# GpSimd's exponent steps as 64-bit integer adds, and its other arithmetic on VectorE

## The chip, the core and the metric

The kernel runs on one core of a Trainium2 chip. A core has five engines with instruction queues of their own: TensorE (PE in the profile, its weight loads PEld) multiplies matrices into PSUM; ScalarE (ACT) computes exponentials and GELU; VectorE (DVE) does elementwise work and empties PSUM; GpSimd (POOL) does elementwise work in SBUF; SyncE (SP) issues DMAs. The metric is the device time of one execution in microseconds. Three runs of the kernel before took 747.74, 748.66 and 748.88 us; the median is 748.66 us.

## What is computed

A token mixer with 2048 tokens of 512 numbers. One branch is softmax attention with 32 heads of 16 numbers each; the other is a small MLP with shifted channels; a gate mixes the two.

```python
def reference(A_x, A_wqkv, A_wo, B_x, B_w1, B_w2, B_w3, B_w4, gate_w):
    ...
        scores = jnp.einsum("bhqd,bhkd->bhqk", q, k) * (Dh ** -0.5)
        p = _softmax(scores, axis=-1)
        o = jnp.einsum("bhqk,bhkd->bhqd", p, v)
        return (lambda x, *d: x.transpose(*d))(o, 0, 2, 1, 3).reshape(B, S, D) @ wo
    ...
        h = _gelu(_layernorm(x, axis=-1) @ w1)
        ...
        x1 = x + hs
        h2 = _gelu(_layernorm(x1, axis=-1) @ w3) @ w4
        return x1 + h2
    x = A_x
    g = _sigmoid((x * gate_w).sum(-1, keepdims=True))
    a = _A_ref(x, A_wqkv, A_wo)
    b = _B_ref(x, B_w1, B_w2, B_w3, B_w4)
    return g * a + (1 - g) * b
```

The scores are 32 matrices of 2048 x 2048 numbers, and the exponential of each of them is the bulk of the elementwise work.

## The kernel before

**Units and blocks.** The attention is cut into 32 units: 512 queries (a chunk `c`) times four heads (`u`). A unit has 16 key tiles of 128 keys, and for each of them one block of 128 x 512 scores per head: 64 blocks, 2048 in all. A score matmul uses 32 rows of the array and an attention matmul 32 columns, so that up to four of a kind run beside each other.

**Two ways to the exponential.** Most blocks lie two or three together in a PSUM tile `stage`, and one ScalarE instruction (`expo`, L1228) takes the exponentials into `ring`; TensorE then multiplies them with the values (`attend_block`, L1241). The other blocks go four by four (a key tile's four heads, in the text a *quad*) through integer arithmetic, in `whole` (L1024). Each block is scored into a PSUM tile `dsc`; VectorE adds a constant and writes int16 (`dump`, L1048): the bits of a bfloat16 number near the exponential. For a better value the sum of four such numbers is taken, each with a shifted exponent and its own weight: three *steps* (`step`, L1090) make the shifted copies of the 128 x 2048 int16 tile, on VectorE (L1113) or on GpSimd (L1111), and TensorE multiplies all four terms with the values, weighted (`vw`) or plain (`vp`). So a quad has up to four dumps, three steps and four attention groups, where ScalarE's way has one attention group.

**Slots.** After the first 34, a score slot has three blocks: three for ScalarE, or two for ScalarE and one for a quad. Two `stage` tiles alternate. The MLP's matmuls, the projections and the output products are fitted between the slots (`job_run`, `proj`, L301), a few matmuls at a time; where nothing is at hand, TensorE multiplies by a tile of zeros (`fill`, L1565).

**A planner writes the order.** Python code at the end (`pe_option`, `option`, `run`) simulates the four engines at build time with a cost for each operation and appends each instruction to its engine's queue in the order of that simulation. On the chip the queues run in that order, with semaphore waits between engines. The costs stand in the `post` calls: 0.157 + 0.533 a block for a dump (L1158), 0.69 for a step on VectorE, 1.9 on GpSimd (`offer`, L1133), 1.28 for a scaling of an output on GpSimd (L1344).

**The limits.** `RULES` (L171) gives limits for each unit, with `USUAL` (L170) for the rest. `DLIM` is how far VectorE's planned backlog may reach when a block is still given to a quad (L777); `MAXD` how many blocks of a unit may go that way; `CHAINS` how many quads may be open. A step is offered to both engines (`offer`, L1142): GpSimd takes it if VectorE's backlog is at least `BACK` and the quad has fewer than `PMAX` steps on GpSimd; VectorE takes it whenever it comes to it. The first step of a quad always goes to VectorE (`opens`, L1125).

**The shared port.** The planner keeps GpSimd's operations and those of VectorE that are posted as `shared` apart in time (L1585, L1591-1593), and `behind` (L264) makes GpSimd's instruction wait for the last such VectorE instruction.

**GpSimd's other work.** The normalized rows `xn` (`norm`, L438), the inverse roots for the two layer norms (`root`, L427 to L430), the second half of `qT` (`odd`, L357), the weighted values `vw` (`weigh`, L366), the scaling of each unit's output by its denominators (`scale`, L1353; the last three units on VectorE, L1351), the gate's last step (`affine`, L486), and one of the last four output tiles (`gate_act`, L1455 to L1469).

Of the kernel before, what the change touches and what calls it, by code (L numbers as in the profile page):

```python
# [33 lines left out]
def kernel(  # L34
# [126 lines left out]
    for j in range(4):  # L161
# [8 lines left out]
    USUAL = {'WIDE': 1, 'NEED': 14, 'AHEAD': 12, 'HURRY': 32, 'DLIM': 1.2, 'MANY': 8, 'PTS': 5, 'CHAINS': 2, 'MAXD': 28, 'PMAX': 3, 'BACK': 1.2, 'SHORT': 1}  # L170
    RULES = {  # L171
        1: {'NEED': 22, 'AHEAD': 20, 'HURRY': 8, 'DLIM': 1.5, 'CHAINS': 5, 'PMAX': 1, 'BACK': 0.0, 'SHORT': 2},
        2: {'NEED': 8, 'AHEAD': 8, 'HURRY': 14, 'DLIM': 0.9, 'MANY': 4, 'PTS': 7, 'CHAINS': 3, 'MAXD': 20, 'PMAX': 2, 'BACK': 0.9, 'SHORT': 3},
        3: {'NEED': 16, 'AHEAD': 20, 'PTS': 6, 'BACK': 0.6},
        4: {'PTS': 7, 'BACK': 0.9},
        5: {'PTS': 4},
        6: {'HURRY': 14, 'MANY': 6, 'MAXD': 24, 'PMAX': 1},
        10: {'NEED': 16, 'AHEAD': 20, 'HURRY': 18, 'DLIM': 2.5, 'MANY': 10, 'PTS': 7, 'MAXD': 24, 'PMAX': 2, 'BACK': -1, 'SHORT': 2},
        12: {'NEED': 32, 'MANY': 6, 'BACK': 0.9},
        13: {'NEED': 12, 'HURRY': 24, 'MANY': 6, 'SHORT': 2},  # L180
        16: {'NEED': 8, 'AHEAD': 16, 'HURRY': 8, 'DLIM': 1.8, 'MANY': 10, 'PTS': 6, 'CHAINS': 3, 'BACK': 0.3},
        17: {'DLIM': 0.6, 'CHAINS': 5},
        18: {'AHEAD': 24, 'HURRY': 0, 'MANY': 6, 'PTS': 4, 'CHAINS': 5, 'SHORT': -1},
        20: {'HURRY': 8, 'MANY': 3},
        22: {'NEED': 10, 'AHEAD': 8, 'HURRY': 8, 'DLIM': 2.5, 'PTS': 3, 'PMAX': 1, 'BACK': 0.6, 'SHORT': -1},
        23: {'NEED': 28, 'AHEAD': 8, 'DLIM': 0.9, 'MANY': 6, 'PTS': 3, 'CHAINS': 5, 'MAXD': 20, 'PMAX': 1, 'BACK': 1.6, 'SHORT': -1},
        24: {'NEED': 18, 'MANY': 6},
        25: {'NEED': 10, 'AHEAD': 16, 'HURRY': 0, 'DLIM': 3.0, 'MANY': 5, 'CHAINS': 3, 'PMAX': 1, 'BACK': 1.6, 'SHORT': 3},
        26: {'NEED': 20, 'AHEAD': 20, 'HURRY': 18, 'MANY': 5, 'PTS': 6, 'CHAINS': 3, 'MAXD': 20, 'PMAX': 2, 'BACK': 0.6, 'SHORT': 2},
        27: {'CHAINS': 4},  # L190
        28: {'NEED': 20, 'AHEAD': 8, 'HURRY': 64, 'DLIM': 0.6, 'MANY': 6, 'PTS': 6, 'CHAINS': 4, 'BACK': 0.6, 'SHORT': 4},
        29: {'NEED': 12, 'AHEAD': 24, 'HURRY': 24, 'MANY': 6, 'PTS': 6, 'CHAINS': 5, 'MAXD': 20, 'PMAX': 2, 'BACK': 1.6, 'SHORT': 2},
        30: {'NEED': 28, 'HURRY': 8, 'DLIM': 1.5, 'MANY': 5, 'CHAINS': 4, 'MAXD': 16, 'BACK': 1.6, 'SHORT': 0},
        31: {'NEED': 16, 'AHEAD': 8, 'HURRY': 4, 'DLIM': 0.9, 'MANY': 10, 'PTS': 4, 'CHAINS': 5, 'MAXD': 20, 'PMAX': 1},
# [29 lines left out]
    GAP = 0.3  # L224
    AGE = 4.0
# [117 lines left out]
    def q_proj(c, G):  # L343
# [4 lines left out]
        def fn(end):  # L348
            qT = qpool.tile([P, 2, CH], BF16, tag="qT", name="qT")
            qTs[(c, G)] = qT  # L350
            nc.vector.tensor_scalar(out=qT[:, 0, :], in0=ps[:], scalar1=QS, scalar2=None, op0=ALU.mult)  # L351
            at["q", c, 2 * G] = end
            post("pool", 1, 0.69, odd, end + 0.04)

        def odd(end):
            qT = qTs[(c, G)]
            behind(nc.gpsimd.tensor_scalar(out=qT[:, 1, :], in0=qT[:, 0, :], scalar1=second[:], scalar2=0.0, op0=ALU.mult, op1=ALU.add))  # L357
# [5 lines left out]
    def weigh(t, half, end):  # L363
        heads = slice(half * H // 2, (half + 1) * H // 2)
        for i in range(2):
            nc.gpsimd.tensor_scalar(out=vw[t][:, i, heads, :], in0=vp[t - 1][:, heads, :], scalar1=WEIGHTS[i + 2], scalar2=0.0,  # L366
                                    op0=ALU.mult, op1=ALU.add)
        at["vw", half] = end

    def v_proj(t, half):  # L370
# [13 lines left out]
        def fn(end):  # L384
            nc.vector.tensor_copy(out=dst[:, heads, 1:DH + 1], in_=ps[:, 0:width].rearrange("p (h d) -> p h d", d=DH))
# [17 lines left out]
    offsets = [const.tile([P, NT], F32, name=f"offset{n}") for n in range(2)]  # L403
# [5 lines left out]
    def ln_stats(n, t):  # L409
# [12 lines left out]
        def plus(end):  # L422
            post("pool", 0, 1.9, root, end + 0.04)

        def root(end):
# [3 lines left out]
            nc.gpsimd.tensor_tensor(out=offsets[n][:, tt], in0=mvs[n][:, tt, 0], in1=rstds[n][:, tt], op=ALU.mult)  # L429
            nc.gpsimd.tensor_scalar(out=offsets[n][:, tt], in0=offsets[n][:, tt], scalar1=-1.0, scalar2=0.0, op0=ALU.mult, op1=ALU.add)  # L430

        aside(0.17, plus)

    def norm(n, c):
        def normed(t):
            def fn(end):
                xn = xnpool.tile([P, D], BF16, tag="xn", name="xn")
                behind(nc.gpsimd.tensor_scalar(out=xn[:], in0=x_sb[t][:], scalar1=rstds[n][:, t:t + 1],  # L438
                                               scalar2=offsets[n][:, t:t + 1], op0=ALU.mult, op1=ALU.add))
# [4 lines left out]
        for t in range(4 * c, 4 * c + 4):  # L444
            post("pool", 1, 0.775, normed(t), all_at(("rstd", n, c), "xnfree"))
# [39 lines left out]
    def affine(end):  # L485
        nc.gpsimd.tensor_scalar(out=g_fin[:], in0=g_t[:], scalar1=0.5, scalar2=0.5, op0=ALU.mult, op1=ALU.add)  # L486
# [1193 lines left out]
```

## Time and profile before

| what | us |
|---|---|
| median of three runs | 748.66 |
| profiled execution, its own time | 748.4 |
| its span, from the first to the last instruction | 746.6 |
| GpSimd busy | 339.3 |
| steps on GpSimd, 123 of them | 233.7 |
| steps on VectorE, 303 of them | 207.9 |
| exponentials on ScalarE, 683 instructions | 679.5 |

Busy times of an engine are unions of its instructions' spans. Neighbouring instructions of one engine overlap in part, so an engine's rate is read from the starts of instructions that follow each other, not from their durations. The granted TensorE clock was 1.0 throughout.

### The profile page before, as it was taken

How to read it: one execution, taken by the hardware profiler on the slowest of the kernel's cores; microseconds unless marked ns; L12 is line 12 of the kernel's file. 1: busy time of each engine (PE TensorE's matmuls, PEld its weight loads, DVE VectorE, ACT ScalarE, POOL GpSimd, SP SyncE). 2: the span in 40 equal slices, each digit the busy share in tenths (PEclk: the TensorE clock that was granted, in tenths of full speed). 3: DMA queues.
4: the chain of work that ended last, by engine and by line, in shares of the span. 5: the costliest groups of instructions: out<-in, count | busy, mean ns of one | idle time of the engine just before them, and what ended most of it. 6: DMA issues, size and time to landing. Idle time of an engine off the chain costs nothing.

```text
span 746.6 us, 23400 instructions
## 1 busy us (share of the span) xinstructions
PE 730.8 (98%) x9866; PEld 230.9 (31%) x9866; DVE 683.6 (92%) x1178; ACT 729.8 (98%) x731; POOL 339.3 (45%) x295
## 2 busy tenths in 40 slices
PE   8999999999999999999999999999999999999997
PEld 4333332322332333332222332222322222322232
DVE  5799999999999998689999989999799999999994
ACT  6999999999999999999999999999999999999995
POOL 3734426444455456325564533454335455345420
PEclk9999999999999999999999999999999999999999
DMA  9400006201130060050001020000201000000011
GB/s 197 124 17 13 13 21 104 47 26 41 34 119 21 18 142 10 21 49 16 20 28 34 14 47 18 19 12 15 56 25 33 6 21 20 26 18 20 15 34 42
DMA packets 52306, 29.03 MB, mean 39 GB/s; under 512 B 36712, under 2 KB 47720, under 8 KB 52200
## 3 DMA queue, kind: packets, MB, share of 16 engines
q1 hardware_dynamic: 51240, 27.00, 15.1%
q8 instruction: 77, 1.26, 0.7%
q10 hardware_dynamic: 960, 0.52, 0.2%
q14 instruction: 29, 0.24, 0.1%
HBM read 17.17 MB, written 2.35 MB: 26 GB/s over the span
## 4 chain that ended last, share of the span: by engine, by line
PE 45%; ACT 41%; issue 10%; DVE 4%; DVEq 0%; ACTq 0%
ACT ring L1228 35%; PE acc L1241 16%; PE stage L831 14%; PE ps L301 6%; ACT pt L1228 3%; PE ps_o L301 2%; PE ps_y L301 2%; PE stage L301 1%; ACT g2T L1205 1%; DVE quad L1048 1%; ACT hT L1205 1%; ACT g2T L1208 1%; DVE xT L1048 1%; PE acc L301 1%; PE ps_q L301 1%
## 5 line engine op out<-in xcount | busy, mean ns | idle before, releaser
L1228 ACT ACTIVATE ring<-stage 128x1024 bf16<-128x1024 f32 (+1 forms) x649 | 648.3, 1159 | 1.9 <-PE dsc L831 0.5
L831 PE MATMUL stage<-qT,kT 32*128 32x512 bf16 (+2 forms) x1530 | 269.1, 380 | 6.0 <-ACT ring L1228 3.1
L831 PE MATMUL dsc<-qT,kT 16*128 16x512 bf16 (+1 forms) x542 | 208.2, 384 | 0.1
L831 PEld LDWEIGHTS <-kT 32*128 32x128 bf16 (+1 forms) x2072 | 77.0, 91 | 278.4 <-issue 250.9
L1048 DVE TENSOR_SCALAR quad<-dsc 128x512 int16<-128x512 f32 x235 | 155.1, 683 | 7.5 <-PE dsc L831 6.5
L1241 PE MATMUL acc<-ring,vp 128*17 128x512 bf16 (+3 forms) x1436 | 133.1, 378 | 1.3 <-DVE accsb L1402 0.5
L1111 POOL TENSOR_SCALAR quad<-quad 128x2048 int16<-128x2048 int16 x36 | 68.4, 1901 | 67.9 <-DVE quad L1113 22.9
L1048 DVE TENSOR_SCALAR more<-dsc 128x512 int16<-128x512 f32 x129 | 85.4, 683 | 5.5 <-PE dsc L831 4.5
L1048 DVE TENSOR_SCALAR xT<-dsc 128x512 int16<-128x512 f32 x122 | 80.5, 683 | 3.1 <-PE dsc L831 2.6
L1241 PEld LDWEIGHTS <-vp 128*17 128x17 bf16 (+1 forms) x2640 | 56.4, 89 | 81.4 <-issue 62.2
L301 PE MATMUL ps<-w,g2T 128*32 128x512 bf16 x896 | 70.2, 383 | 0.0
L1111 POOL TENSOR_SCALAR more<-more 128x2048 int16<-128x2048 int16 x20 | 38.0, 1900 | 56.8 <-DVE quad L1113 30.7
L1353 POOL TENSOR_TENSOR oT<-accsb,bcs 128x512 bf16<-128x512 f32 x29 | 37.1, 1279 | 44.6 <-DVE quad L1113 22.2
L301 PE MATMUL ps_y<-xnT,w 128*32 128x512 bf16 x704 | 54.8, 383 | 0.3 <-DVE qT L351 0.3
L1113 DVE TENSOR_SCALAR quad<-quad 128x2048 int16<-128x2048 int16 x61 | 45.6, 748 | 0.7 <-PE acc L1241 0.7
L1241 PE MATMUL acc<-quad,vp 128*17 128x512 bf16 x492 | 45.8, 381 | 0.0
L1111 POOL TENSOR_SCALAR xT<-xT 128x2048 int16<-128x2048 int16 x16 | 30.4, 1901 | 33.1 <-DVE xT L1113 7.0
L1241 PE MATMUL acc<-quad,vw 128*17 128x512 bf16 x468 | 45.2, 381 | 0.0
L1111 POOL TENSOR_SCALAR more<-quad 128x2048 int16<-128x2048 int16 x14 | 26.6, 1901 | 27.7 <-DVE quad L1113 8.1
L1048 DVE TENSOR_SCALAR lent<-dsc 128x512 int16<-128x512 f32 x56 | 37.2, 682 | 1.5 <-PE dsc L831 1.2
L1241 PEld LDWEIGHTS <-vw 128*17 128x17 bf16 x1136 | 27.8, 88 | 33.7 <-issue 25.7
L301 PEld LDWEIGHTS <-w 128*32 128x32 bf16 x1152 | 26.1, 95 | 35.3 <-issue 19.4
(146 smaller groups left out, 943.8 us busy)
## 6 DMA issues: line engine op xcount, KB each, us to landing
bcs<-rec_d SPq DMA_DIRECT2D x31, 256.0 KB
w<-in_B_w_dram SPq DMA_DIRECT2D x2, 1792.0 KB
x_sb<-in_A_x_dram SPq DMA_DIRECT2D x14, 128.0 KB
oT<-oT SPq DMA_DIRECT2D x112, 16.0 KB
out_dram<-ot SPq DMA_DIRECT2D x12, 128.0 KB
w<-in_B_w_dram SPq DMA_DIRECT2D x2, 512.0 KB
wkv<-in_A_wqkv_dram SPq DMA_DIRECT2D x1, 512.0 KB
wo_all<-in_A_wo_dram SPq DMA_DIRECT2D x8, 64.0 KB
```

What stands on the lines that cost most here:

```text
L301: nc.tensor.matmul(out[j:j + 32, :], lhsT=lhsT[:, j:j + 32], rhs=rhs, tile_position=(0, j), **kwargs)
L831: nc.tensor.matmul(out, lhsT=kT[G][32 * j:32 * j + K, cc, o:o + P], rhs=qTs[(c, G)][32 * j:32 * j + K, a, lo:hi], start=True, stop=True, t ...
L1048: nc.vector.tensor_scalar(out=bits[:, r:r + wide, :], in0=dsc.rearrange("p (a c) -> p a c", c=CH), scalar1=SHIFT, scalar2=LOWEST, op0=ALU. ...
L1111: behind(nc.gpsimd.tensor_scalar(out=to, in0=base["tile"], scalar1=1.0, scalar2=shift, op0=ALU.mult, op1=ALU.add))
L1113: fast["ins"] = nc.vector.tensor_scalar(out=to, in0=base["tile"], scalar1=shift, scalar2=None, op0=ALU.add)
L1205: nc.scalar.activation(out=part, in_=part, func=ACT.Gelu_apprx_tanh)
L1208: nc.scalar.activation(out=dst, in_=stages.pop(k)[:, 0:len(ms) * CH].rearrange("p (a c) -> p a c", c=CH), func=ACT.Gelu_apprx_tanh)
L1228: nc.scalar.activation(out=pt[:, 0:w], in_=stages.pop(k)[:, 0:w], func=ACT.Exp, scale=LN2 / 128.0)
L1241: nc.tensor.matmul(accs[n][32 * j:32 * j + M, lo:hi], lhsT=lhsT, rhs=p, start=(kt == 0), stop=(kt == NT - 1), skip_group_check=True, tile_ ...
L1353: behind(nc.gpsimd.tensor_tensor(out=oT, in0=tiles["accsb"][:], in1=tiles["bcs"][:], op=ALU.mult))
```

## The change

Five things change.

1. A step on GpSimd is one `int64_add` over the tile seen as 512 64-bit words per partition, with the shift repeated in the four 16-bit lanes, in place of a `tensor_scalar` over 2048 int16 elements. Every lane stays positive, so nothing is carried from lane to lane. The planner's cost for it is 1.07 in place of 1.9.
2. GpSimd's other arithmetic goes to VectorE: `odd`, `weigh`, `norm`, `affine`, every `scale` and the last tile's `gate`. The second layer norm's inverse roots are computed on VectorE by an integer first guess and four Newton rounds (19 small instructions for four tiles of rows); the first layer norm's stay on GpSimd, without the two instructions for `offset`.
3. `scale` is posted to VectorE without the mark `shared`.
4. VectorE leaves a step to GpSimd if GpSimd is free less than `KEEP` = 0.6 us after VectorE, as long as the quad has fewer than `PMAX` = 3 steps there.
5. The limits of units 1 to 31 are one set.

```diff
+        1: {'NEED': 10, 'AHEAD': 8, 'HURRY': 0, 'DLIM': 0.6, 'MANY': 10, 'PTS': 6, 'CHAINS': 6, 'MAXD': 24, 'BACK': 0.6, 'SHORT': 0, 'KEEP': 0.6},
...
+    PSTEP = 1.07
...
+    def words(tile):
+        return tile.rearrange("p a c -> p (a c)").bitcast(mybir.dt.int64)
...
-            post("pool", 1, 0.69, odd, end + 0.04)
+            post("vector", 1, 0.41, odd, end + 0.04, True)
...
-                post("pool", 1, 0.95, lambda end: weigh(t, half, end), end + 0.04)
+                post("vector", 1, 0.5, lambda end: weigh(t, half, end), end + 0.04, True)
...
+        def newton(end):
+            at["rstd", n, t // 4] = end
+            y, z = rstds[n][:, tt], root_z[:]
+            half = root_x[:]
+            nc.vector.tensor_scalar(out=half, in0=mvs[n][:, tt, 1], scalar1=EPS, scalar2=None, op0=ALU.add)
+            nc.vector.tensor_scalar(out=z.bitcast(I32), in0=half.bitcast(I32), scalar1=1, scalar2=None, op0=ALU.logical_shift_right)
+            nc.vector.tensor_scalar(out=y.bitcast(I32), in0=z.bitcast(I32), scalar1=-1.0, scalar2=float(MAGIC), op0=ALU.mult, op1=ALU.add)
+            for _ in range(4):
+                nc.vector.tensor_tensor(out=z, in0=y, in1=y, op=ALU.mult)
+                nc.vector.tensor_tensor(out=z, in0=z, in1=half, op=ALU.mult)
+                nc.vector.tensor_scalar(out=z, in0=z, scalar1=-0.5, scalar2=1.5, op0=ALU.mult, op1=ALU.add)
+                nc.vector.tensor_tensor(out=y, in0=y, in1=z, op=ALU.mult)
+        if n:
+            aside(1.6, newton)
+        else:
+            aside(0.17, plus)
...
-                behind(nc.gpsimd.tensor_scalar(out=xn[:], in0=x_sb[t][:], scalar1=rstds[n][:, t:t + 1],
-                                               scalar2=offsets[n][:, t:t + 1], op0=ALU.mult, op1=ALU.add))
+                fast["ins"] = nc.vector.tensor_scalar(out=xn[:], in0=x_sb[t][:], scalar1=mvs[n][:, t, 0:1],
+                                                      scalar2=rstds[n][:, t:t + 1], op0=ALU.subtract, op1=ALU.mult)
...
-                behind(nc.gpsimd.tensor_scalar(out=to, in0=base["tile"], scalar1=1.0, scalar2=shift, op0=ALU.mult, op1=ALU.add))
+                behind(nc.gpsimd.int64_add(out=words(to), in0=words(base["tile"]), in1=int(shift) * 0x0001000100010001))
...
-            offer("pool", 1.9, end)
+            offer("pool", PSTEP, end)
...
+                elif chain["pool"] < rule("PMAX") and free["pool"] < free["vector"] + rule("KEEP"):
+                    return None
...
-            post("vector" if late else "pool", 0 if late else 3, 0.68 if late else 1.28, scale, lambda: landed if oroom or u % 2 else None, True)
+            post("vector", 0 if late else 3, 0.68, scale, lambda: landed if oroom or u % 2 else None)
...
-            if j:
-                post("vector", -5 * r + (r == 0), 0.75, gate, free["pe"] + 0.2)
-            else:
-                post("act", 1, 0.6, gate_act, free["pe"] + 0.2)
+            post("vector", -5 * r + (r == 0), 0.75, gate, free["pe"] + 0.2)
```

More of the change, by code (lines that the diff above doesn't have):

```diff
@@ L402 @@
     rstds = [const.tile([P, NT], F32, name=f"rstd{n}") for n in range(2)]
-    offsets = [const.tile([P, NT], F32, name=f"offset{n}") for n in range(2)]
+    MAGIC = 0x5f3759df
+    root_x, root_z = (const.tile([P, 4], F32, name=f"root_{k}") for k in "xz")
     xns = {}
@@ L1349, in scale @@
             oT = oroom.popleft() if padded else npool.tile([P, CH], BF16, tag="oT", name="oT")[:]
[L1350 to L1353 removed]
+            nc.vector.tensor_tensor(out=oT, in0=tiles["accsb"][:], in1=tiles["bcs"][:], op=ALU.mult)
             at["o", c, u] = end
```

81 lines of the change are left out of this document (36 added, 45 removed).

## The prediction

> **What bounds the kernel now.** I read the page first, its busy times and the engines' shares of the chain that ended last.
>
> ```profile
> PE 730.8 (98%) x9866; PEld 230.9 (31%) x9866; DVE 683.6 (92%) x1178; ACT 729.8 (98%) x731; POOL 339.3 (45%) x295
> PE 45%; ACT 41%; issue 10%; DVE 4%; DVEq 0%; ACTq 0%
> ```
>
> TensorE and ScalarE share the chain, and VectorE is nearly full too. Busy shares alone don't say who has room, so the second view is ScalarE's groups by shape, and the third a stretch of its timeline.
>
> ```profile
> L1228 ACT ACTIVATE ring<-stage 128x1024 bf16<-128x1024 f32 x535 | 505.0, 1082 | 1.5 <-PE dsc L831 0.5
> L1228 ACT ACTIVATE ring<-stage 128x1536 bf16<-128x1536 f32 x114 | 163.0, 1517 | 0.5 <-PE stage L831 0.3
> L1228 ACT ACTIVATE pt<-stage 128x1024 bf16<-128x1024 f32 x34 | 31.4, 1091 | 0.6 <-PE stage L831 0.5
> 359.86 8.50 ACT L1228 ACTIVATE ring<-stage 128x1024 bf16<-128x1024 f32 x9
> ```
>
> Idle time ahead of the exponentials is 2.6 us in all. Nine of them in 8.50 us with a last one of 1.08 start every (8.50 - 1.08) / 8 = 0.93 us. A third block costs 1517 - 1082 = 0.435 us more. At these prices ScalarE's 569 instructions of two blocks and 114 of three need 569 x 0.93 + 114 x 1.365 = 685 us; the rest of its 729.8 busy us is GELUs and table loads. **ScalarE sets the time, and the time falls only where blocks are taken from it**: 4 x 0.435 = 1.74 us for each further quad. The blocks that it has: 535 x 2 + 114 x 3 + 34 x 2 = 1480 of 2048, so 568 blocks, 142 quads, go the other way.
>
> Who could take more? The fourth view is the windows, one stage of the first half and one of the second, then the same stages for the multiplications by zeros alone (TensorE).
>
> ```profile
> 150.00:200.00 50.00, 49.64 (x641) 14.82 (x640) 49.01 (x83) 49.98 (x52) 22.62 (x18) 1.00 0.17 38
> 350.00:400.00 50.00, 49.52 (x661) 14.25 (x657) 48.27 (x80) 49.85 (x51) 27.31 (x19) 1.00 0.10 31
> ```
>
> ```profile
> 150.00:200.00 50.00, 4.95 (x52) 1.00 0.17 38
> 350.00:400.00 50.00, 0.39 (x4) 1.00 0.10 31
> 0.00:747.00 747.00, 28.77 (x328) 1.00 0.16 39
> ```
>
> VectorE (third engine column) is busy 49.0 and 48.3 of 50 us: it has no room in either half. TensorE has some in the first half, where it multiplies by zeros 13 times (52 instructions, four beside each other), and almost none in the second (once). So VectorE's relief is what the change can turn into quads, and in the second half TensorE may not allow it.
>
> **The change part by part.** The steps first: their number and price on the two engines, the prices of GpSimd's other work, and the starts of VectorE's steps.
>
> ```profile
> 0.00:747.00 747.00, 207.89 (x303) 1.00 0.16 39
> 0.00:747.00 747.00, 233.74 (x123) 1.00 0.16 39
> L1111 POOL TENSOR_SCALAR quad<-quad 128x2048 int16<-128x2048 int16 x36 | 68.4, 1901 | 67.9 <-DVE quad L1113 22.9 <-DVE xT L1113 15.9 <-DVE more L1113 12.0
> L1353 POOL TENSOR_TENSOR oT<-accsb,bcs 128x512 bf16<-128x512 f32 x29 | 37.1, 1279 | 44.6 <-DVE quad L1113 22.2 <-DMA bcs<-rec_d 7.5 <-DVE mv L417 6.1
> L438 POOL TENSOR_SCALAR xn<-x_sb,rstd,offset 128x512 bf16<-128x512 bf16 x32 | 24.4, 772 | 13.2 <-issue 5.7 <-DVE lent L1113 4.5 <-DVE quad L1113 1.9
> L366 POOL TENSOR_SCALAR vw<-vp 128x272 bf16<-128x272 bf16 x24 | 12.1, 504 | 8.1 <-DVE g_raw L390 7.0
> L357 POOL TENSOR_SCALAR qT<-qT,second 128x512 bf16<-128x512 bf16 x15 | 10.4, 692 | 11.4 <-DVE qT L351 6.2 <-DVE more L1113 2.6 <-DVE quad L1113 1.2
> 269.20 0.69 DVE L1113 TENSOR_SCALAR xT<-quad 128x2048 int16<-128x2048 int16 x1
> 269.80 0.69 DVE L1113 TENSOR_SCALAR more<-more 128x2048 int16<-128x2048 int16 x1
> 270.40 0.69 DVE L1113 TENSOR_SCALAR quad<-quad 128x2048 int16<-128x2048 int16 x1
> ```
>
> 303 + 123 = 426 steps are three for each of 142 quads, as counted above. A VectorE step takes 0.60 us of the queue.
>
> *Price of a 64-bit step.* No row shows one. Bounds: 0.69 us (L357, as many elements as there are words, a quarter of the bytes) and 1.90 us (L1111, the same bytes). The planner's costs for the operations above are 1.9, 1.28, 0.775 and 0.69 against 1.901, 1.279, 0.772 and 0.692 in the rows, so its 1.07 for the new one is likely a measured figure too, and it lies between the bounds. I take it.
>
> *Steps off VectorE.* The first step of a quad stays there: 142. Of the other 284 the new rule leaves to GpSimd those for which GpSimd is free within 0.6 us of VectorE. GpSimd would be busy 40% of the time, so I take nine in ten, 256; VectorE keeps 170. That is 133 fewer, 133 x 0.60 = 79.8 us off VectorE. Ends: all 284 (161 fewer, 96.6 us) and six in ten (90 fewer, 54 us). GpSimd: 339.3 - 233.7 - 84.0 (the four other rows) + 256 x 1.07 = 296 us; it has the room.
>
> *Work onto VectorE.* Rows of VectorE for the nearest operations:
>
> ```profile
> L1351 DVE TENSOR_TENSOR oT<-accsb,bcs 128x512 bf16<-128x512 f32 x2 | 1.4, 684 | 0.4 <-DMA bcs<-rec_d 0.4
> L390 DVE COPY g_raw<-ps_v 128x1 f32<-128x1 f32 x16 | 2.4, 147 | 0.0
> L1113 DVE TENSOR_SCALAR xT<-xT 128x2048 int16<-128x2048 int16 x20 | 13.8, 694 | 0.2
> L385 DVE CAST vp<-ps_v 128x256 bf16<-128x256 f32 x32 | 13.3, 415 | 3.5 <-PE ps_v L301 3.3
> L1504 DVE TENSOR_SCALAR qT<-ps_q,mask 128x256 bf16<-128x256 f32 x1 | 0.5, 484 | 0.7 <-PE ps_q L1499 0.7
> L417 DVE BATCH_NORM_AGGREGATE mv<-st 128x2 f32<-128x6 f32 x32 | 5.6, 174 | 0.2
> ```
>
> The 29 scalings: 684 ns is 0.60 in the queue (0.09 overlaps, as for the steps), 17.4 us. `xn` and `qT`, 47 of 512 columns from SBUF: between one column (147) and 2048 (694), on the line 0.28 us, with 0.07 added for scalars read from memory (484 against 415) and 0.09 overlapped: 0.26, 12.2 us (ends 0.06 and 0.60: 3 and 28 us). `vw`, 24 of 272 columns: 0.13, 3.1 us. The Newton rounds, 4 x 19 instructions, each on the result of the one before: nothing overlaps, 0.174 and a little for the hand-over, 0.20: 15.2 us, where the planner has 4 x 1.6 = 6.4. Together 47.9 us.
>
> *The unmarked scalings.* `scale` reads two SBUF tiles and is no longer kept apart from GpSimd. If the two cannot run together, it waits for the step under way: from nothing to 1.07 us each, 0 to 31 us. GpSimd busy 40% of the time and half a step on average would be 0.21; I take 0.25, 7.3 us. The Trainium skill, "SBUF — State Buffer", section "Who interferes with whom", speaks against the edit: a VectorE instruction with two SBUF inputs contends with a GpSimd instruction that reads SBUF, and the loser blocks wholly. By that rule the 7.3 us stay in, without it they go, which is worth 2.7 us at the end; the two L1351 above can't show it.
>
> *What that buys.* Net relief 79.8 - 47.9 - 7.3 = 24.6 us of VectorE. A further quad costs it four dumps and 1.2 steps:
>
> ```profile
> L1048 DVE TENSOR_SCALAR quad<-dsc 128x512 int16<-128x512 f32 x235 | 155.1, 683 | 7.5 <-PE dsc L831 6.5
> ```
>
> (4 + 1.2) x 0.60 = 3.1 us; and it shortens the run by 1.74, of which VectorE was using 92%: 1.6. So 24.6 / 4.7 = 5.2 quads at an equally full VectorE: **-9.1 us**. TensorE pays three more attention groups a quad, 0.22 us each by their starts:
>
> ```profile
> 299.72 0.39 PE L1241 MATMUL acc<-more,vp 128*17 128x512 bf16 x4
> 299.94 0.39 PE L1241 MATMUL acc<-quad,vw 128*17 128x512 bf16 x4
> ```
>
> 5.2 x 0.66 = 3.4 us, which the 82 groups of zeros (18 us) hide in the first half. Without that cover it is the first rival.
>
> *What the Newton rounds hold up.* Each run of 19 takes 3.8 us of VectorE's queue where 1.6 are planned. Behind it stand dumps, and the score slot after next waits for them, then ScalarE. 4 x 2.2 = 8.8 us if all is passed on, 0 if VectorE was ahead; I take a third: **+2.9 us**.
>
> *The end.* The last work is the gate of the last tiles.
>
> ```profile
> 740.67 1.27 POOL L1461 TENSOR_TENSOR ring<-ring,parts 128x512 bf16<-128x512 f32 x1 [21.12 <-ACT ring L1458]
> 740.74 2.07 DVE L1451 SCALAR_TENSOR_TENSOR ring<-end,g_fin,parts 128x512 bf16<-128x512 f32 x3
> ```
>
> Four in place of three on VectorE, 0.69 each with overlap 0.66: **+0.7 us** (at worst; nothing if the fourth fits ahead).
>
> *The one set of limits.* I cost it at nothing, as the count of quads follows from VectorE's room above; its price if it is not so is the second rival.
>
> Sum: 746.6 - 9.1 + 2.9 + 0.7 = 741.1 us of span; the execution's 748.4 is 1.8 longer than its span, so 742.9, **743 us**. That execution is 0.26 us under the median of 748.66. With all steps on GpSimd, no port wait and Newton at 6.4 us: (96.6 - 39.1) / 4.6 = 12.5 quads, -21.8 us, 727; with `xn` and `qT` at their lower end two quads more, 724.
>
> **The rivals.** *No room on TensorE.* The zeros are gone after 300 us, so TensorE can carry more attention groups only in the first half. Then half of the 9.1 us comes, and with the 3.6 lost above the time is 748.4 - 4.5 + 3.6 = 747.5, no change. For it: the two window rows above. Against it: the MLP's matmuls can slide forward into the room.
>
> *A backlog limit that refuses quads* (slower). `DLIM` is now 0.6 everywhere; a single dump of 0.68 in the queue exceeds it. Before, units 17 and 28 had 0.6 and units 24 and 29 had 1.2; their dumps, in windows between the copies of the accumulators (line 1048), in that order:
>
> ```profile
> 401.20:422.50 21.30, 11.72 (x18) 1.00 0.07 21
> 656.60:678.10 21.50, 11.96 (x19) 1.00 0.05 16
> 563.40:584.80 21.40, 13.02 (x20) 1.00 0.10 31
> 678.10:700.60 22.50, 15.09 (x24) 1.00 0.07 20
> ```
>
> 0.86 dumps per us under 0.6, 1.00 under 1.2: 14% fewer. If the 71 quads of the second half lose that, 10 x 1.74 = 17.4 us, and with 3.6 the time is 769; with part of it made good by the freed VectorE, 765. It decides as soon as quads fall below 140, where the 3.6 us are no longer paid for. Against it: a less loaded VectorE seldom has 0.6 us of backlog.
>
> *A dear or late 64-bit step.* TensorE's order is fixed with a step of 1.07 and 0.25 of hold. At 1.9 each of 256 steps is up to 0.58 late, at most 148 us; it begins to hurt above 1.3. The Trainium skill, "GPSIMD Engine Reference", section "2.1 Instruction dispatch", has about 6 us for the first call of a freshly loaded routine, which by an estimate from that page would make 749 if nothing hid it; no run here shows it, and GpSimd idles 7.17 us ahead of its first step (row below).
>
> ```profile
> 44.63 1.90 POOL L1111 TENSOR_SCALAR lent<-quad 128x2048 int16<-128x2048 int16 x1 [7.17 <-DVE quad L1113]
> ```
>
> *The steps don't move.* GpSimd still takes a step only when VectorE's backlog is 0.6 or more. If VectorE kept its 303, the 47.9 us would cost 48 / 4.7 = 10 quads: +17.4, with 3.6 769 us.
>
> **How the numbers follow.** Forecast, with its better cases, 54%; no room on TensorE 14%; backlog limit 24%; dear step 5%; steps stay 3%. Under 0.2% (1.5 us) a measurement can't tell the time from no change. So faster 0.54, same 0.14, slower 0.32. The range reaches from the best case of the forecast (724, a little under for unknown prices) to the backlog rival: 722 to 768; perhaps 4% lie below and 14% above.
>
> **What would show it.** Right: about 147 quads (588 dumped blocks), ScalarE's instructions of three blocks fewer than 114, some 256 rows of GpSimd at about 1.07 us, VectorE's steps near 170 to 180, VectorE still about 92% busy. Wrong: fewer than 140 quads; TensorE waiting for GpSimd's steps; idle time of ScalarE well over 2.6 us, above all at the Newton rounds; more multiplications by zeros, which would say that TensorE, too, was left with nothing to do.

## The result: slower by 2.8%

The changed kernel took 770.16 us (median of four runs, 768.23 to 793.91) beside 748.27 us for the kernel before on the same chip: a ratio of 1.0284, 95% interval 1.0248 to 1.032. The forecast was 743 us. Executions more than 1.5% above the fastest of their kernel, all at a lower granted clock, are left out of the ratios: here the one of 793.91 us, and below five of ten near 771 us of the run with one round alone and two of four, 777 and 783 us, of the run in five pieces. The profiled execution took 768.44 us with a span of 766.7, which is 20.1 us longer than before.

The page's busy times and shares of the chain, of the changed kernel, then ScalarE's exponentials by shape (count, busy us, mean ns, idle us ahead of them and what ended it):

```profile
PE 736.3 (96%) x9833; PEld 222.9 (29%) x9834; DVE 662.2 (86%) x1220; ACT 723.7 (94%) x728; POOL 319.5 (42%) x338
PE 52%; ACT 26%; DVE 12%; issue 8%; DMA 1%; POOL 1%; SPq 0%; DVEq 0%; ACTq 0%; POOLq 0%
```

```profile
L1256 ACT ACTIVATE ring<-stage 128x1024 bf16<-128x1024 f32 x549 | 518.4, 1059 | 16.1 <-PE dsc L857 14.9
L1256 ACT ACTIVATE ring<-stage 128x1536 bf16<-128x1536 f32 x98 | 141.0, 1481 | 5.8 <-PE stage L857 5.5
L1256 ACT ACTIVATE pt<-stage 128x1024 bf16<-128x1024 f32 x34 | 31.6, 1084 | 2.2 <-PE stage L857 2.2
```

ScalarE was relieved as forecast: 549 x 2 + 98 x 3 + 34 x 2 = 1460 blocks, so 588 blocks or 147 quads go the other way, five more than before, and its busy time falls by 6.1 us. But it stands idle 24.1 us ahead of the exponentials, where it stood 2.6, nearly all of it waiting for score matmuls.

The steps on GpSimd, those on VectorE and the multiplications by zeros, each a window over the whole span with busy us and count; then the operations that moved to VectorE:

```profile
0.00:766.70 766.70, 308.02 (x292) 0.98 0.16 38
```

```profile
0.00:766.70 766.70, 102.81 (x149) 0.98 0.16 38
```

```profile
0.00:766.70 766.70, 21.41 (x236) 5.91 (x236) 0.21 (x1) 0.98 0.16 38
```

```profile
L1378 DVE TENSOR_TENSOR oT<-accsb,bcs 128x512 bf16<-128x512 f32 x31 | 25.5, 824 | 0.0
L464 DVE TENSOR_SCALAR xn<-x_sb,mv,rstd 128x512 bf16<-128x512 bf16 x32 | 12.6, 404 | 0.0
L369 DVE TENSOR_SCALAR qT<-qT,second 128x512 bf16<-128x512 bf16 x15 | 5.1, 343 | 0.0
L378 DVE TENSOR_SCALAR vw<-vp 128x272 bf16<-128x272 bf16 x24 | 4.8, 246 | 0.0
```

GpSimd made 292 steps at 308.02 / 292 = 1.05 us, and VectorE's steps fell from 303 to 149. So the steps moved as the change says. The time went in two other places.

**The start.** GpSimd's timeline of the changed kernel, then of the kernel before, then ScalarE's first exponential in both:

```profile
0.87 0.21 POOL masks.py:197 MEMSET ident<- 128x128 bf16 x1
9.16 0.28 POOL masks.py:199 TENSOR_SCALAR_AFFINE_SELECT ident<-ident 128x128 bf16<-128x128 bf16 x1 [8.08 <-issue]
...
14.61 1.94 ACT L1256 ACTIVATE pt<-stage 128x1024 bf16<-128x1024 f32 x2 [0.50 <-PE stage L857]
```

```profile
1.14 0.29 POOL masks.py:199 TENSOR_SCALAR_AFFINE_SELECT ident<-ident 128x128 bf16<-128x128 bf16 x1
...
9.07 1.94 ACT L1228 ACTIVATE pt<-stage 128x1024 bf16<-128x1024 f32 x2 [0.50 <-PE stage L831]
```

GpSimd stands 8.08 us ahead of the identity matrix, "issue" meaning that nothing in the profile releases it. The transposes need that matrix, and the first exponential is 5.5 us late.

**The Newton rounds.** One of the four places, on VectorE (first and last of 19 instructions), TensorE and ScalarE:

```profile
291.09 0.17 DVE L446 TENSOR_SCALAR root_x<-mv 128x4 f32<-128x4 f32 x1
...
294.68 0.16 DVE L453 TENSOR_TENSOR rstd<-rstd,root_z 128x4 f32<-128x4 f32 x1
294.75 0.68 DVE L1074 TENSOR_SCALAR quad<-dsc 128x512 int16<-128x512 f32 x1
```

```profile
292.59 0.39 PE L857 MATMUL stage<-qT,kT 16*128 16x512 bf16 x2
295.49 0.37 PE L857 MATMUL dsc<-qT,kT 16*128 16x512 bf16 x1 [2.51 <-DVE quad L1074]
```

```profile
297.02 1.02 ACT L1256 ACTIVATE ring<-stage 128x1024 bf16<-128x1024 f32 x1 [2.76 <-PE dsc L857]
```

VectorE is held from 291.09 to 294.75. The dump behind it frees the PSUM tile that TensorE's next score needs, TensorE stands 2.51 us, and ScalarE then 2.76. What follows is in the windows (TensorE's busy time and matmuls, then the granted clock):

```profile
292.50:295.90 3.40, 0.89 (x11) 1.00 0.65 128
295.90:313.00 17.10, 17.03 (x130) 0.50 0.06 19
319.80:323.20 3.40, 1.81 (x26) 1.00 0.00 0
323.20:330.00 6.80, 5.40 (x45) 0.50 0.03 10
```

After the stand TensorE runs at half its clock for 17.1 us, and after the fourth place, where it stood 2.99 us, for another 6.8. ScalarE waits for it again and again in these stretches. At the first two places TensorE stood 2.37 and 2.15 us, and no half clock followed.

### The profile page after: what moved, and what is told of

Read it like the earlier page. It is cut to its first block, busy times and chain, and to the rows that moved or that the text cites. A ratio compares the mean times of both kernels' runs of the same rounds, so it can differ in the third digit from the quotient of the medians.

```text
span 766.7 us, 23523 instructions
## 1 busy us (share of the span) xinstructions
PE 736.3 (96%) x9833; PEld 222.9 (29%) x9834; DVE 662.2 (86%) x1220; ACT 723.7 (94%) x728; POOL 319.5 (42%) x338
## 4 chain that ended last, share of the span: by engine, by line
PE 52%; ACT 26%; DVE 12%; issue 8%; DMA 1%; POOL 1%; SPq 0%; DVEq 0%; ACTq 0%; POOLq 0%
ACT ring L1256 23%; PE acc L1269 18%; PE stage L857 16%; PE ps L313 7%; PE ps_y L313 3%; PE stage L313 3%; ACT pt L1256 3%; DVE more L1074 3%; PE ps_o L313 2%; DVE xT L1074 2%; PE ps_q L313 1%; DVE quad L1074 1%; DMA xT<-in_A_x_dram 1%; PE dsc L857 1%; DVE quad L1139 1%
## 5 line engine op out<-in xcount | busy, mean ns | idle before, releaser
L857 PE MATMUL stage<-qT,kT 16*128 16x512 bf16 (+3 forms) x1514 | 271.2, 384 | 11.0 <-DVE more L1074 5.1
L857 PE MATMUL dsc<-qT,kT 16*128 16x512 bf16 (+1 forms) x558 | 216.4, 388 | 2.8 <-DVE quad L1074 2.5
L857 PEld LDWEIGHTS <-kT 32*128 32x128 bf16 (+1 forms) x2072 | 73.2, 91 | 295.9 <-issue 269.0
L1074 DVE TENSOR_SCALAR quad<-dsc 128x512 int16<-128x512 f32 x206 | 138.0, 685 | 22.0 <-PE dsc L857 20.2
L1074 DVE TENSOR_SCALAR more<-dsc 128x512 int16<-128x512 f32 x177 | 118.2, 684 | 17.4 <-PE dsc L857 15.7
L1137 POOL INT64_ADD quad<-quad x68 | 72.5, 1066 | 73.2 <-PE acc L1269 15.1
L1137 POOL INT64_ADD quad<-more x28 | 29.9, 1071 | 59.9 <-DVE xT L1139 17.6
L1137 POOL INT64_ADD more<-more x29 | 30.2, 1040 | 49.2 <-DVE quad L1139 16.1
L1137 POOL INT64_ADD quad<-xT x25 | 25.9, 1040 | 31.0 <-DVE quad L1139 13.6
L1137 POOL INT64_ADD xT<-xT x28 | 30.5, 1090 | 13.7 <-DVE more L1139 7.1
L313 PEld LDWEIGHTS <-w 128*32 128x32 bf16 x1152 | 24.6, 96 | 38.3 <-issue 25.4
L1137 POOL INT64_ADD xT<-quad x20 | 21.0, 1053 | 30.9 <-DVE quad L1139 13.1
```

The source lines that it names most:

```text
L313: nc.tensor.matmul(out[j:j + 32, :], lhsT=lhsT[:, j:j + 32], rhs=rhs, tile_position=(0, j), **kwargs)
L857: nc.tensor.matmul(out, lhsT=kT[G][32 * j:32 * j + K, cc, o:o + P], rhs=qTs[(c, G)][32 * j:32 * j + K, a, lo:hi], start=True, stop=True, t ...
L1074: nc.vector.tensor_scalar(out=bits[:, r:r + wide, :], in0=dsc.rearrange("p (a c) -> p a c", c=CH), scalar1=SHIFT, scalar2=LOWEST, op0=ALU. ...
L1137: behind(nc.gpsimd.int64_add(out=words(to), in0=words(base["tile"]), in1=int(shift) * 0x0001000100010001))
```

## The experiments

Two theories at first. A: VectorE, held longer than planned by the rounds, makes TensorE stand, and the half clock follows. B: the one set of limits orders the work worse. Beside them the start had to be explained.

**One Newton round in place of four**, in the changed kernel. The planned cost stays, so every other instruction and its order are the same; the roots are less exact.

```diff
-            for _ in range(4):
+            for _ in range(1):
```

> The changed kernel with one Newton round in place of four at the second layer norm (7 small VectorE instructions in a row in place of 19; the normalized rows are less exact). The planner's cost is left at 1.6 us, so that every queue has the same order as in the changed kernel otherwise. Theory A (VectorE held for 3.9 us at four places, behind which TensorE stands still, and the half clock that follows): 7 x 0.20 = 1.4 us fits in the planned 1.6, the waits and the half clock go, 768.4 - 18 = about 750 us, granted clock 1.00. Theory B (the one set of limits makes a worse order; the Newton rounds matter little): 764 us or more. The load at the start stays in both.

The five runs in the ratio took 749.36 to 753.57 us, ratio 1.004 [1.0021, 1.0059]; the profiled execution 749.36 us (span 747.6). In it the clock stayed full between start and end, and the idle time by shape is

```profile
L1256 ACT ACTIVATE ring<-stage 128x1024 bf16<-128x1024 f32 x549 | 517.9, 1062 | 3.6 <-PE dsc L857 2.4
L1256 ACT ACTIVATE ring<-stage 128x1536 bf16<-128x1536 f32 x98 | 140.8, 1484 | 0.9 <-PE stage L857 0.7
L1256 ACT ACTIVATE pt<-stage 128x1024 bf16<-128x1024 f32 x34 | 31.5, 1087 | 1.8 <-PE stage L857 1.8
```

6.3 us in place of 24.1. With the order of the work unchanged, three rounds fewer are worth 766.7 - 747.6 = 19.1 us of span. That is A; what B can still account for is what is left between this kernel and the forecast.

**The kernel before with the 19 instructions**, on scratch tiles, at the same four places and not planned; nothing else of the change.

```diff
+            if n:
+                newton()
```

> The kernel before, with the 19 instructions of the Newton rounds added on scratch tiles at the same four places and not priced in the plan; nothing reads them, and every other instruction and its order are those of before. Theory A: a VectorE held for 3.9 us at each place costs 4 x 3 us of waiting and, where TensorE stands still for over 2 us, the half clock: 760 to 768 us, clock under 1.00. Theory B: 749 to 752 us, clock 1.00.

775.59 us (772.61 to 776.12), ratio 1.037 [1.0353, 1.0387]: 24.2 us of span for 76 small instructions, more than the 12 to 20 expected. Five of the 76 took 0.55 to 1.57 us, each beside a `tensor_scalar` of GpSimd, so that two of the four blocks held VectorE for 5.55 and 5.16 us, the other two for 3.76. The four windows ahead of its four stretches of half clock (TensorE's busy us and matmuls, clock):

```profile
237.10:240.50 3.40, 1.48 (x21) 1.00 0.08 19
261.00:264.40 3.40, 0.81 (x9) 1.00 0.00 0
281.50:284.90 3.40, 0.36 (x8) 1.00 1.50 249
305.40:308.80 3.40, 0.49 (x7) 1.00 0.00 0
```

So the rounds alone can cost as much as the whole loss, in a kernel that has neither the new limits nor 64-bit adds.

**The kernel before with one 64-bit add** where GpSimd idles, near the end; behind it comes that kernel's ordinary addition for the last tile.

```diff
+        nc.gpsimd.int64_add(out=spare64[:].bitcast(mybir.dt.int64), in0=spare64[:].bitcast(mybir.dt.int64), in1=0)
```

> The kernel before, with one 64-bit add on a scratch tile late on GpSimd, where it idles for 21 us ahead of its last instruction. Theory A1 (a program with a 64-bit add begins with a stand of 8 us on GpSimd ahead of the identity matrix, which TensorE's first transposes need): first exponential 5.5 us later, 754 us. Rival (the late start has another cause in the changed kernel): 748 to 749 us.

747.39 us, ratio 0.9995 [0.9985, 1.0004], and the identity matrix at 1.35 us. So a 64-bit add somewhere in the program does not by itself delay the start, and that reading fell. One difference left was the order: here an ordinary instruction comes last on GpSimd, in the changed kernel an add does.

**The identity matrix by DMA**, in the changed kernel: VectorE writes it and two DMAs carry it through DRAM.

```diff
-    make_identity(nc, ident[:])
+    nc.sync.dma_start(out=ident_d.rearrange("(p x) -> p x", x=P + 1), in_=ones[:])
...
+    nc.sync.dma_start(out=ident[:], in_=ident_d[0:P * P].rearrange("(p x) -> p x", x=P))
```

> The changed kernel with the identity matrix made by VectorE memsets and two DMAs through DRAM in place of GpSimd's affine select; all later order is the same. Theory A1: the identity is there at about 5.5 us in place of 9.4, first exponential 3 to 4 us earlier, 765 us at the same clock of 0.984. Rival (the start is bound by a DMA or something else anyway): 768 us, unchanged.

767.8 us, ratio 1.0261 [1.0239, 1.0284]. GpSimd's cast of the matrix, which waits for the DMA, starts at 6.90 us, later than the 5.5 expected, and the first exponential starts at 12.48 us: 2.1 us of the start came back. The interval of the ratio overlaps that of the changed kernel, so a gain in time is not shown by this run. The stand itself did not go: 8.06 us of it, again with "issue", now lie on GpSimd ahead of its first `tensor_scalar`, at 15.24 us, while its memsets and the cast ran without it. So it belongs to GpSimd and not to the identity matrix.

**An ordinary GpSimd instruction behind the last add**, in the changed kernel.

```diff
     def finish_all():
+        nc.gpsimd.tensor_scalar(out=last[:], in0=mhalf[:], scalar1=1.0, scalar2=EPS, op0=ALU.mult, op1=ALU.add)
```

> The changed kernel with one small ordinary GpSimd instruction (128x4) behind its last 64-bit add, where GpSimd idles for 18 us; all other instructions and their order are the same. Theory S (what is left behind): the 8.08 us in which GpSimd stands ahead of the identity matrix are a change of its code, needed because the execution before ended with the 64-bit add's code in place; the kernel before with one 64-bit add followed by an ordinary instruction began without the stand (0.29 us). Then the identity matrix is made at about 1.3 us, the first exponential starts at about 9.1 in place of 14.6 us, and the time falls by 5 to 5.5 us, to 763 to 765. Rival (program): the stand belongs to any program with many 64-bit adds; then nothing changes: first exponential at 14.6 us, 768 to 770. Both expect the half clock at about 296 and 323 us to stay.

764.39 us (763.33 to 767.56), ratio 1.0217 [1.0197, 1.0236]. GpSimd's timeline at both ends of it, and ScalarE's first exponential:

```profile
1.35 0.29 POOL masks.py:199 TENSOR_SCALAR_AFFINE_SELECT ident<-ident 128x128 bf16<-128x128 bf16 x1 [0.29 <-POOL ident masks.py:197]
...
742.11 1.04 POOL L1138 INT64_ADD xT<-xT  x1
750.22 0.19 POOL L1487 TENSOR_SCALAR last<-mhalf 128x4 f32<-128x4 f32 x1 [7.07 <-issue]
...
8.31 1.02 ACT L1257 ACTIVATE pt<-stage 128x1024 bf16<-128x1024 f32 x1 [0.50 <-PE stage L858]
```

The stand has moved to the end, where 7.07 us of it lie under the last output tiles, the first exponential starts 6.3 us earlier, and the span fell by 766.7 - 761.4 = 5.3 us. That is less than 6.3. This trace has half clock behind all four places, 3.4, 3.4, 17.1 and 6.8 us, where the changed kernel has it behind two, which may be why. That is what is to be seen if an execution starts with the code that the one before left; the loading of code itself has no row in the profile. The Trainium skill, "GPSIMD Engine Reference", section "2.1 Instruction dispatch", gives about 6 us for the first call of a freshly loaded routine; the two stands here, 8.08 and 7.07 us, are longer, and that they are such a load is not shown.

**Two rounds, with that instruction.** The order is again the same.

```diff
-            for _ in range(4):
+            for _ in range(2):
```

> The instruction at the end as before this, and two Newton rounds in place of four: 11 small VectorE instructions in place of 19, 2.2 us in place of 3.8, at the same four places and at the same planned 1.6 us; all other instructions and their order are the same. Theory A (a VectorE held 3.8 us lets TensorE stand long enough for the half clock): 2.2 us is nearer to the 1.4 us of one round, which showed no half clock, than to 3.8; TensorE's stands stay under 2 us, the clock stays full, and the time is that with one round (747.6 us of span) less 5.5 us at the start and some 4 x 0.8 at most for the longer hold: a span of 742 to 745, a time of 744 to 747, a ratio to the kernel before under 1. If the half clock already follows a hold of 2.2 us: 752 to 760. If the start does not move (rival of the run before this): 749 to 752.

750.95 us (744.5 to 752.84), ratio 1.0008 [0.9983, 1.0033]. The twelve runs fall into two groups: four from 744.50 to 745.70 at a mean clock of 0.999 or 1.0, eight from 750.54 to 752.84 at 0.988 to 0.991; the forecast had 744 to 747 or 752 to 760, not both. The profiled execution is of the second kind:

```profile
281.90:285.30 3.40, 2.40 (x25) 1.00 0.68 130
285.30:288.70 3.40, 3.40 (x29) 0.50 0.08 17
```

A window in which TensorE stood 1.0 of 3.4 us was followed by 17.07 us at half clock. A hold of 2.2 us thus lies on the border: the same order of work comes out 5 to 8 us apart, with the clock.

**The rounds in five pieces** of 3, 4, 4, 4 and 4 instructions, between which the planner may put other work; all four rounds, and the ordinary instruction at the end.

```diff
-            aside(1.6, newton)
+            aside(0.69, newton)
+            for _ in range(4):
+                aside(0.89, again)
```

> All four Newton rounds, but as five pieces (3, 4, 4, 4 and 4 instructions) at 0.69 and 4 x 0.89 us, between which the planner may put dumps and steps; the instruction at the end as well. The plan comes out with 145 quads in place of 147, which is 2 x 1.74 = 3.5 us by ScalarE's prices. Theory A (it is the unbroken 3.8 us that hurts, not the 15 us of work): no half clock, ScalarE's idle time ahead of the exponentials near that with one round (6.3 us); one round's span 747.6 + 3.5 - 5.5 + 1 for the rest of the work = 746 to 748. Rival W (the work on VectorE hurts, wherever it lies): 15 us of VectorE's queue come back as time, and the kernel stays as the run with four rounds and the instruction at the end, 762 to 766.

764.63 and 764.73 us, ratio 1.0214 [1.0196, 1.0231]: the number of rival W, and far from the 746 to 748 of theory A. The half clock did fall, from the 30.7 us of the run with the instruction at the end to 10.2, not counting the last 10 us of the span. VectorE's and GpSimd's timelines show one cost that the pieces have instead:

```profile
236.83 0.71 DVE L455 TENSOR_TENSOR root_z<-rstd 128x4 f32<-128x4 f32 x1
237.58 0.98 DVE L456 TENSOR_TENSOR root_z<-root_z,root_x 128x4 f32<-128x4 f32 x1
238.59 0.17 DVE L457 TENSOR_SCALAR root_z<-root_z 128x4 f32<-128x4 f32 x1
```

```profile
236.49 1.04 POOL L1144 INT64_ADD xT<-more  x1 [3.81 <-DVE quad L1146]
237.50 1.04 POOL L1144 INT64_ADD quad<-more  x1
```

Small instructions that meet a 64-bit step end with it: at 237.54 and 238.56, the steps at 237.53 and 238.54. Thirteen of the 76 took 0.4 to 1.04 us in place of 0.17. In the four blocks of 19 of the changed kernel there were two, 0.30 and 0.90 us. Besides, the two quads fewer cost 3.5 us by ScalarE's prices, and 12.7 us lie behind the last exponential in place of 7.4. Which of these decides was not tested alone.

**The limits of the kernel before**, with two rounds and the instruction at the end: the old table for units 1 to 31, `KEEP` 0.6 throughout.

> Two Newton rounds and the instruction at the end, but the limits of the kernel before for units 1 to 31 (KEEP 0.6 throughout). The plan gives 138 quads in place of 147. Theory B (the one set of limits orders the work worse, and cost the change its gain): the time is at or under that of the same kernel with the one set. Against it, ScalarE's prices: 9 quads fewer x 1.74 = 15.7 us more, so 757 to 763; the one set is then worth some 15 us and no part of the loss.

778.8 us, ratio 1.0407 [1.039, 1.0424], above both forecasts. Against the profiled execution with the one set (span 750.5) it is 25.4 us longer: 138 quads in place of 147 by the plan, which is 15.7 us at ScalarE's prices, and 21.1 us between the last exponential and the end, against 7.4, where output products and VectorE's additions to them stand one behind another. These two make 29.4 us, so one of them is priced too high, or something else came back. B is refuted as far as the old table goes: with the new costs it is much worse. Whether some third set would be better than the one set was not tried.

**Plans that know the length.** Two rounds at 2.29 us, and four at 3.9, kept apart from GpSimd's steps by the planner; then the five pieces kept apart. All with the instruction at the end.

```diff
-            aside(1.6, newton)
+            aside(2.29, newton, None, True)
```

> Two Newton rounds (11 instructions), planned at 2.29 us in place of 1.6 and kept apart from GpSimd's steps by the planner, with the instruction at the end. The plan has 147 quads. Two Newton rounds at 1.6 gave 744.5 to 745.7 us where the clock stayed full and 750.5 to 752.8 where a stand of TensorE of 0.93 us at 283 us was followed by 17.07 us of half clock. Theory A with the port (VectorE late against the plan makes the stands; part of the lateness is a small instruction held for a whole 64-bit step): a plan that knows the length leaves no stand of 0.9 us, the clock stays full in all runs, 743 to 746, ratio 0.993 to 0.998. Rival (the hold itself makes stands, planned or not): half clock in some runs, median 750 to 752.

> All four Newton rounds in one piece as in the changed kernel, but planned at 3.9 us in place of 1.6 and kept apart from GpSimd's steps; the instruction at the end. The plan has 145 quads (3.5 us against 147). Theory A in its narrow form (a wrong price: the plan puts dumps where VectorE is not free): with the right price TensorE's order has other work there, ScalarE's idle time comes near 7 us, the clock stays full or nearly so, 748 to 751. Rival H (a hold of 3.9 us can't be covered, whatever the plan knows: two score tiles alternate): stands and half clock stay, 760 to 766.

> The five pieces of the run with the rounds in pieces, now kept apart from GpSimd's steps by the planner; the instruction at the end; 145 quads as there. In that run 13 of the small instructions took 0.4 to 1.04 us in place of 0.17, each while GpSimd made a 64-bit step, 8 us in all. Theory P (port: a small instruction that meets a 64-bit step waits for most of it, and the pieces meet more of them than one block does): nearly all small instructions take 0.2 us, the stands of TensorE of 0.7 us and more go from six to one or none, the time falls from 764.6 to 747 to 751. Rival W (the work itself on VectorE): 762 to 766 as before.

They took 755.72, 759.88 and 760.63 us, ratios 1.0094 [1.0079, 1.0109], 1.0153 [1.0125, 1.0181] and 1.0166 [1.0145, 1.0187]: all slower than the theories had it, and the first is outside its rival's range too. In the first the half clock was down to 3.4 us (mean clock 0.997), and still TensorE stood 1.77 us at one place. Four rounds at their true price gain about 3.5 us of span on the unpriced ones (757.9 against 761.4), with two quads fewer. The first of the three also shows what else a new plan brings, on ScalarE's timeline:

```profile
351.61 1.02 ACT L1257 ACTIVATE ring<-stage 128x1024 bf16<-128x1024 f32 x1 [6.15 <-PE acc L1270]
```

This stand ends 53 us after the last root, with TensorE busy on the MLP's matmuls. In the last of the three, ten small instructions still met a 64-bit step although the planner keeps them apart, and 17.8 us lie behind its last exponential. Each of these changes moves the whole order, by as much as the effect in question, so the three can't tell whether a well-planned hold could be covered. That stays open.

**One round, and two rounds in nine instructions**, both with the instruction at the end and the changed kernel's order. The first is less exact; in the second `scalar_tensor_tensor` does a round in three instructions.

```diff
+                nc.vector.scalar_tensor_tensor(out=z, in0=z, scalar=-0.5, in1=half, op0=ALU.mult, op1=ALU.mult)
+                nc.vector.scalar_tensor_tensor(out=y, in0=z, scalar=1.5, in1=y, op0=ALU.add, op1=ALU.mult)
```

> One Newton round of the four (7 small instructions, about 1.4 us where 1.6 are planned; the roots are less exact, to about 0.2%) and the ordinary GpSimd instruction at the end; all else and the order as in the changed kernel. Theory (the two losses, a VectorE held longer than planned and the stand at the start, are all that kept the forecast from coming true): the span of 747.6 us with one round less the 5.5 to 6.3 us at the start, 741.5 to 742.5; a time of 743 to 745, ratio 0.993 to 0.997, the clock full in all runs. Rival (another loss is left in the change, the one set of limits or the unmarked scalings): 747 to 751, ratio 0.999 or more.

> Two Newton rounds of the four in 9 instructions in place of 11 (each round's four are put into three), the instruction at the end, all else and the order as in the changed kernel: VectorE is held 1.8 us at a time. One round (1.4 us) showed no half clock, two rounds in 11 instructions (2.2 us) showed 17 us of it in 8 of 12 runs. Theory A: the shorter hold lies nearer to one round; most runs keep the full clock, 743 to 746, and the median falls below 748. Rival: half clock in most runs as with 11 instructions, median 750 to 752.

One round: 742.18 us (741.69 to 742.58), ratio 0.9917 [0.9904, 0.993]. Nine instructions: 743.81 us (743.16 to 751.09), ratio 0.9963 [0.9933, 0.9992]; five of its seven runs lie at 743.16 to 744.81. Both are faster than the kernel before, by 0.8% and 0.4%. Of the run with one round, the page's busy times, ScalarE's groups, and the scalings on VectorE:

```profile
PE 726.0 (98%) x9833; PEld 222.6 (30%) x9834; DVE 653.2 (88%) x1172; ACT 722.0 (97%) x728; POOL 319.1 (43%) x339
```

```profile
L1257 ACT ACTIVATE ring<-stage 128x1024 bf16<-128x1024 f32 x549 | 517.9, 1062 | 3.6 <-PE dsc L858 2.4
L1257 ACT ACTIVATE ring<-stage 128x1536 bf16<-128x1536 f32 x98 | 140.8, 1484 | 0.9 <-PE stage L858 0.7
L1257 ACT ACTIVATE pt<-stage 128x1024 bf16<-128x1024 f32 x34 | 31.4, 1093 | 0.6 <-PE stage L858 0.5
```

```profile
L1379 DVE TENSOR_TENSOR oT<-accsb,bcs 128x512 bf16<-128x512 f32 x31 | 25.6, 825 | 0.0
```

With its span of 740.8 us the difference can be split. The change with one round, and without the stand at the start, is worth 740.8 - 746.6 = -5.8 us; three further rounds cost 761.4 - 740.8 = 20.6; the start costs 766.7 - 761.4 = 5.3. These are steps from one run to the next, so they add up to the measured +20.1 whatever the causes are. A test is the other order, through the run with one round alone: there the rounds cost 766.7 - 747.6 = 19.1 us and the start 747.6 - 740.8 = 6.8. So each size holds to about 1.5 us.

## Why the prediction was wrong

**The step that failed is "What the Newton rounds hold up".** It foresaw the place and the mechanism: 19 instructions of VectorE's queue in 3.8 us where 1.6 are planned, dumps behind them, then the score slot, then ScalarE. The place shown above took 294.75 - 291.09 = 3.66 us, the fourth 4.63 with two of its instructions held by a 64-bit step. But the size was taken as 2.9 us, a third of an upper end of 8.8, the excess of the four holds over the plan. The three further rounds measured 19.1 to 20.6 us. Two things make the difference. The excess makes TensorE stand, and TensorE then ran at half speed for up to 17 us, which the prediction has no term for. And nearer to all of the excess than a third of it was passed on. An estimate of the two shares: with two rounds, the three executions at a mean clock of 0.988 took 7.6 us longer on average than the four at full clock, for 17.07 us at half clock in the profiled one, so some 0.44 us for each us of it. The 30.7 us at half clock of the run with four rounds and the instruction at the end are then about 13.5 of its 20.6 us, and about 7 are the holds themselves. In windows from 300 to 310 us (columns PE, PEld, DVE, ACT, POOL, then the clock) the changed kernel and the one with one round compare so:

```profile
300.00:310.00 10.00, 10.00 (x77) 1.69 (x78) 6.79 (x14) 6.74 (x7) 2.97 (x3) 0.50 0.02 2
```

```profile
300.00:310.00 10.00, 9.00 (x127) 3.06 (x123) 9.45 (x19) 9.38 (x9) 2.08 (x2) 1.00 0.04 9
```

TensorE is busy all the time in the first, with 77 matmuls in place of 127, and ScalarE works 6.7 us in place of 9.4. The page of before shows a clock of 1.0 throughout, and the forecast speaks of the clock nowhere.

**The start was missing from the sum.** The rival of a dear or late step had the price of a change of GpSimd's code, but only ahead of the first 64-bit step. There it is hidden, as was argued: the first step waits 9.49 us for VectorE's anyway. A stand at the start of the execution was in no term; it cost 5.3 to 6.8 us.

**The quads came out right, in part by luck.** Five more were forecast and five came; ScalarE's work fell by 6.1 to 7.8 us, where 9.1 were forecast for the time. But 292 steps of the 294 that could go went to GpSimd, not nine in ten, so 154 steps or 92 us left VectorE in place of 79.8. By the prediction's rule that would have bought 2.6 further quads. They did not come, and VectorE is busy 88% in the kernel with one round, not 92: the plan left room there. Two errors met: more relief than forecast, and less of it used. What set the number at 147 wasn't tried.

**Right:** the price of a 64-bit step (1.05 us against 1.07); the work onto VectorE but for the rounds' effect; the wait of the unmarked scalings: 824 ns against 684 before, so 0.14 us each, 4.3 us for 31, where 7.3 was the estimate for 29. Singly, 12 of the 31 took 0.76 to 1.52 us, each started while a 64-bit step ran; those that started ahead of a step kept 0.68, and the step beside them took 1.30 to 1.50 in place of 1.04, so GpSimd pays a part too. The Trainium skill's rule of "SBUF — State Buffer", section "Who interferes with whom", was borne out by these, and by the small `tensor_tensor` instructions that ended with GpSimd's steps. Small `tensor_scalar` instructions with one tile as input ended with them as well, such as the one of 0.90 us. **Wrong in sign:** the end, taken at +0.7 us; from the last exponential to the end it is 7.4 us after and 9.0 before.

**The rivals:** a lack of room on TensorE did not decide. Up to the 16th copy of an accumulator VectorE made 270 dumps in place of 261, behind it 288 in place of 281, so the further quads lie in both halves, and the kernel with one round is faster. Its premise was too strong as well: of the 328 multiplications by zeros before, 80 lie behind 300 us, where it says that they are gone. The backlog limit did not bring the quads below 140, the sign that was named for it: they are 147. Whether it kept them from being more is part of what wasn't tried. The steps moved.

Without the hold's 2.9 us the forecast's span is 738.2 us. One round and a free start measured 740.8, 2.6 us more; ScalarE's idle time ahead of the exponentials is 2.5 us more than before, 5.1 against 2.6, which would account for it.

## What to carry to other kernels

A chain of small dependent instructions costs the queue behind it its whole length, and if TensorE waits there, the granted clock can multiply that: price such a chain instruction by instruction from neighbouring starts (0.20 us each here), shorten it until no stand of TensorE near 1 us remains, and look at the clock behind every stand. Where GpSimd gets a new kind of instruction, look at both ends of the program, and let an instruction of the kind that the start needs come last. An experiment that keeps the order of the instructions says more than one for which a planner makes a new order.

## What the hardware did that was not expected

The half clock starts and ends on a grid: the stretches in the traces are 3.41, 6.83, 10.24 and 17.07 us long, multiples of 3.413, and the two starts in the changed kernel, 295.9 and 323.2 us, are 27.3 us or eight times 3.413 apart. The Trainium skill, "TensorE: Matmul & The Clock Gate", section "What's actually happening", has a free-running window of 3413 ns, which agrees, and puts the lower clock after an idle window; here windows in which TensorE was busy 0.36 to 2.40 of 3.4 us were followed by it, as the rows above show, and the measurement decides. Busy time alone doesn't decide, for in the changed kernel these two were not followed by it:

```profile
244.70:248.10 3.40, 1.97 (x30) 1.00 0.00 0
278.80:282.20 3.40, 2.16 (x29) 1.00 0.21 74
```

The stand of 2.37 us at the first place is the same in the run with the instruction at the end, which starts 6 us earlier, and there 3.41 us of half clock followed. So it seems to count where a stand falls on the grid; how much idle time it takes was not measured.

In these runs the last kind of instruction on GpSimd goes with how an execution starts: 8.08 us of standing ahead of the identity matrix where a 64-bit add comes last, 0.29 where an ordinary one does. One instruction that was added at the end moved it.
